# First weights split behind the first norm, longer load runs, and V's layer norm tiles in another order

## The chip, the cores and the metric

One Trainium2 chip, one of its cores. The metric is device microseconds of one execution of the program; the number given for a kernel is the median of its runs. Each core has five engines with a queue of their own: TensorE (PE, whose weight loads the profile shows apart as PEld), VectorE (DVE), ScalarE (ACT), GpSimd (POOL) and SyncE (SP, which here issues nearly all DMAs).

## What is computed

Three layers over 8 batches of 576 tokens with 512 features, all in float32:

```python
# 1. linear attention, 8 heads of 64, no softmax, then an RMS norm per head
kv  = einsum('bhsd,bhse->bhde', k, v)
out = einsum('bhsd,bhde->bhse', q, kv)
x   = out / sqrt(mean(out * out, -1) + 1e-6) * g_norm      # -> [8, 576, 512]
# 2. four experts of one causal attention head each, the best two of each token weighted
q, k, v = x @ wq[e], x @ wk[e], x @ wv[e]
a   = softmax(causal(q @ k.T / 8));  ye = a @ v @ wo[e];  x2 = sum of w[e] * ye
# 3. gated MLP with a matrix over the sequence
h   = gelu(x2 @ w_in);  u, v = h[..., :512], h[..., 512:]
v_n = (v - mean(v)) / sqrt(var(v) + 1e-6) * g_ln
out = x2 + (u * (w_sg @ v_n + b_sg)) @ w_out
```

## The kernel before

The program runs in two phases. Phase 1 does layers 1 and 2 batch by batch, phase 2 does layer 3. TensorE multiplies in fp32r, a faster format with fewer bits, so that each float32 operand that matters is split in a high part and the rest (`whi`/`wlo`, `xhi`/`xlo`), and a product is three matmuls: high by high, high by low, low by high.

The code doesn't issue instructions where it stands. A `Recorder` collects every operation, and its `plan` goes through a list schedule: it has a duration for each kind of operation (`cost`), and of the operations that are ready on an engine it takes the one with the lowest index. The index comes from `streams` and `merge`: each part of a batch (`front`, `norm`, `v`, `qk0`, `qk1`, `attn`), the split of the weights (`wld`, `wts`) and the conversions of phase 2's weights (`conv`, `conv2`) is a generator with a window, a start and an end in units of batches, in the table `OPT["w"]`. A pair in `behind` adds a dependency for the planner alone: the operation is not planned before the marked one. What comes out is one fixed order for each engine, and on the chip each engine goes through its own in that order and waits where an operand is missing. Since one helper (line 465) issues all of it, the profile is read by tiles.

The start, which is batch 0. `load` brings a pair of heads' K and V (tile `kv`, two DMAs) and Q (tile `q`), four pairs a batch; a DMA waits in SP's queue until the one eight before it has landed. `kv` multiplies K by V into `kvps`, `outT` multiplies by Q into `outps`; ACT squares that into `sq`, `stat` sums the squares over a head with a matmul into `statps`. `rstd` takes the root: ACT a logarithm and an exponential, then DVE a Newton step, in tiles `ya`, `yb`, `yc`; the result `y` is put in `rr`, whose upper 16 rows of 32 hold its high part and the lower ones the rest. `norm` spreads `rr` over the features with a matmul by zeros and ones (`bsel_sb`) into `nps`, for batch 0 twice, where the second overwrites the first; DVE multiplies it with `o`, and ACT and DVE or POOL split that into `xhi` and `xlo`. `fetch_weights` loads Q's, K's and V's weights into `wstage` in three pieces, and `split` makes `whi` and `wlo` of them. `vproj` (tile `vps`) and `qk_half` (tile `qkps`) are the projections. Batch 1's `kv` and `outT` follow.

The boundary of the phases. `Phase2.first` is merged with the end of batch 7's attention. It loads the result of phase 1 (`x`, `ends`), the two halves of `w_in` (`load_wi(1)` for V, `load_wi(0)` for U), w_sg (`weights_early`), multiplies four of V's tiles for batch 0 (`vmat`, the gelu waits) and then all U tiles of batches 0 and 1 (`upart`). A gelu is held back until the last exponential of the attention is done, since ACT needs another table for it. `rest` then makes V's gelu and layer norm, `vnorm`, of nine tiles: 0 to 3 are batch 0, 4 holds the last 64 rows of both batches, 5 to 8 are batch 1. A `vnorm` is a gelu on ACT, on DVE the statistics (tile `bs`), a subtraction (`vg`) and the rest after the split (`vn`), and on POOL the power -0.5 (`lny`). After that `spart` multiplies by w_sg, which needs tiles 0 to 4 for batch 0:

```python
for k in range(4):
    ps = self.vmat(0, k)
    (nc.vector.tensor_copy if k % 2 else nc.scalar.copy)(self.raw[:, k, :], ps)
    if k == 3:
        self.load_wi(0)
...
for k in (0, 4, 1, 5, 2, 6, 3, 7, 8):
    self.vnorm(0, k, self.raw[:, k, :] if k < 4 else self.vmat(0, k))
```

From there on phase 2 is one dense stream of matmuls to the end.

Of the kernel before, what the change touches and what calls it, by code (L numbers as in the profile page):

```python
# [27 lines left out]
F32 = mybir.dt.float32  # L28
F32R = mybir.dt.float32r
# [4 lines left out]
OP = mybir.AluOpType  # L34
# [7 lines left out]
E = 4  # L42
# [6 lines left out]
OPT = dict(ob=1, sx=0, pinq=0, dv=0, pin=1, cvb=2, xb=1, ldb=4, hp={}, n1=0, n2=0, f1=0, pa=4, sA=(), dg=0, cost=(1.01, 0.88, 1.22, 1.47, 1.28), avi=1, prb=4, ahb=4, alb=2, qkb=2, ahead=3, w={'attn': (0.177, 1.304), 'qk1': (0.038, 0.221), 'qk0': (-0.557, -0.055), 'v': (-0.518, -0.311), 'front': (-1.553, -1.219), 'norm': (-0.888, -0.788), 'conv': (-0.519, 3.66), 'conv2': (2.908, 6.876), 'wts': (-1.697, -1.585), 'u': (-0.178, 0.89), 'front_0': (-1.676, -1.565), 'v_0': (-1.282, -1.086), 'qk0_0': (-1.221, -1.003), 'qk1_0': (-0.126, -0.047), 'norm_0': (-1.418, -1.388), 'front_1': (-1.649, -1.316), 'norm_1': (-1.133, -0.89), 'v_1': (-0.728, -0.395), 'qk0_1': (-0.41, -0.088), 'wld': (-1.972, -1.907)})  # L49
# [183 lines left out]
class Recorder:  # L233
# [72 lines left out]
    def cost(self, op, outs, ins):  # L306
# [18 lines left out]
        if op.eng == "scalar":  # L325
# [148 lines left out]
class Phase1:  # L474
# [6 lines left out]
    def __init__(self, tc, late, early, ins, wts, gvd, nb):  # L481
        self.tc, self.nc, self.nb, self.gvd, self.wts = tc, tc.nc, nb, gvd, wts
        (self.qT, self.kvp, self.gn, self.wqkvg, self.woT, self.sel, self.bsel, self.mask, self.ident, self.sides) = ins
# [29 lines left out]
    def load(self, n):  # L513
# [4 lines left out]
        kv = self.ld.tile([P, 2, NQ, P], F32, name="kv", tag="kv")  # L518
        q = self.ld.tile([P, S], F32, name="q", tag="q")
        src = self.kvp[b, c]  # L520
# [3 lines left out]
        self.loads[n] = (q, kv[:, 0], kv[:, 1])  # L524
# [10 lines left out]
    def consts(self):  # L535
# [4 lines left out]
        nc.vector.memset(self.eps, 1e-6)  # L540
        self.tri = cst.tile([P, 1, E, E], F32, name="tri")
# [560 lines left out]
class Phase2:  # L1102
# [221 lines left out]
    def first(self):  # L1324
# [159 lines left out]
```

## Time and profile before

| | |
|---|---|
| Median of 3 runs | 805.79 us (805.34 to 806.64) |
| The profiled execution: its own time | 806.44 us |
| Its span, first to last instruction | 804.5 us |
| PE busy | 781.5 us, 97% of the span |
| PEld, DVE, ACT, POOL busy | 85%, 57%, 48%, 38% |
| Mean granted clock of TensorE | 0.994 |

The span is 1.94 us shorter than the execution's own time: what lies before the first and behind the last instruction. A group of instructions stands in the profile as engine, operation, output tile, input tiles, shape, how many, and busy time. In the timeline the bracket at a row's end is how long the engine stood idle before it and what ended that. Trace counts of the plain float32 matmuls (`kvps`, `outps`, `statps`, `nps`'s pairs aside) are twice the program's, as the chip does them in two passes.

### The profile page before, as it was taken

Reading aid. Unit: us, or ns where it says so; the run is one execution under the profiler, and the core shown is the slowest. Engines: PE = TensorE matmul, PEld = TensorE weight load, DVE = VectorE, ACT = ScalarE, POOL = GpSimd, SP = SyncE. Lnnn points to the kernel's source line nnn. Section 1 sums busy time; section 2 is a strip of 40 time slices with the busy share of each in tenths; the row PEclk is TensorE's granted clock in tenths of the full one; section 3 lists DMA queues with packets and bytes.
Section 4 is the critical chain, followed back from the end, with each engine's and each line's share of the span. In section 5 each row is a group of like instructions: output and inputs, shape, how many; then the busy total and the mean of one; then the engine's idle time right before and its main releaser. Section 6 shows DMA issues by size and latency. Waiting matters only on the chain.

```text
span 804.5 us, 16419 instructions
## 1 busy us (share of the span) xinstructions
PE 781.5 (97%) x5944; PEld 684.8 (85%) x5944; DVE 457.7 (57%) x1336; ACT 387.2 (48%) x1018; POOL 309.7 (38%) x419
## 2 busy tenths in 40 slices
PE   4899999999999999999998999999999999999998
PEld 3778788897998979889877898988989898989896
DVE  1767876958657577796558684443536254521230
ACT  1546675665656666676567844323423233322110
POOL 0346784747732558985113341311213121211120
PEclk9799999999999999999999999999999999999999
DMA  9989778685786788365596711203020310001002
GB/s 267 291 227 248 211 209 255 173 238 153 202 230 187 204 229 232 118 197 132 132 264 217 280 53 40 73 26 112 14 99 1 112 27 27 27 27 40 26 28 66
DMA packets 77090, 114.46 MB, mean 142 GB/s; under 512 B 13265, under 2 KB 40593, under 8 KB 77010
## 3 DMA queue, kind: packets, MB, share of 16 engines
q1 hardware_dynamic: 76866, 112.90, 48.6%
q8 instruction: 47, 0.77, 0.4%
q0 software_dynamic: 144, 0.52, 0.2%
q14 instruction: 33, 0.27, 0.1%
HBM read 58.31 MB, written 26.77 MB: 106 GB/s over the span
## 4 chain that ended last, share of the span: by engine, by line
PE 90%; DMA 3%; DVE 2%; POOL 2%; ACT 1%; SPq 1%; issue 0%; ACTq 0%; DVEq 0%; POOLq 0%
PE ps L465 44%; PE qkps L465 12%; PE vps L465 7%; PE scps L465 6%; PE tps L465 5%; PE avps L465 5%; PE outps L465 3%; PE kvps L465 2%; DMA kv<-in_kvp 2%; PE wxps L465 2%; PE nps L465 1%; PE rps L465 1%; PE statps L465 1%; SPq L465 1%; POOL xlo L465 1%; DVE vn L465 1%
## 5 line engine op out<-in xcount | busy, mean ns | idle before, releaser
L465 PE MATMUL ps<-wsh,vn 128*128 128x288 f32 x576 | 120.4, 295 | 0.7 <-ACT vn L465 0.5
L465 ACT ACTIVATE prob<-prob,small 128x128 f32<-128x128 f32 (+4 forms) x160 | 96.0, 601 | 29.7 <-DVE small L465 27.5
L465 PEld LDWEIGHTS ps<-wsh,vn 128*128 128x128 f32 x576 | 94.3, 188 | 1.9 <-ACT vn L465 0.7
L465 POOL TENSOR_TENSOR gl<-g,gh 128x512 fp32r<-128x512 f32 x32 | 41.6, 1299 | 137.7 <-ACT gh L465 94.6
L465 DVE CUSTOM_DVE_ANT_0 prob<-scps,mask_sb 128x128 f32<-128x128 f32 (+4 forms) x160 | 74.2, 469 | 18.1 <-PE scps L465 16.3
L465 POOL TENSOR_TENSOR lny<-lny,mhalf 128x1 f32<-128x1 f32 x36 | 33.8, 939 | 131.6 <-DVE lny L465 131.6
L465 PE MATMUL qkps<-xhi,whi 128*128 128x288 f32 x256 | 79.4, 310 | 0.0
L465 PE MATMUL qkps<-xlo,whi 128*128 128x288 f32 x256 | 76.4, 298 | 0.0
L465 PE MATMUL qkps<-xhi,wlo 128*128 128x288 f32 x256 | 76.4, 298 | 0.0
L465 PE MATMUL ps<-wsl,vn 128*128 128x288 f32 x256 | 75.5, 295 | 0.0
L465 PE MATMUL tps<-id_sb,prob 128*128 128x128 f32 (+2 forms) x480 | 75.3, 260 | 0.1
L465 PE MATMUL scps<-kh,qs 128*128 128x128 f32 (+2 forms) x192 | 65.0, 343 | 0.2 <-ACT aT L465 0.2
L465 PEld LDWEIGHTS tps<-id_sb,prob 128*128 128x128 f32 (+2 forms) x480 | 52.8, 137 | 10.7 <-issue 5.1
L465 PE MATMUL scps<-kl,qs 128*128 128x128 f32 (+2 forms) x192 | 59.0, 311 | 0.0
L465 DVE TENSOR_TENSOR g<-ps,u 128x288 f32<-128x288 f32 x64 | 28.9, 455 | 51.5 <-PE ps L465 50.9
L465 ACT CAST gh<-g 128x512 fp32r<-128x512 f32 x32 | 19.8, 619 | 78.5 <-DVE g L465 60.9
L465 POOL TENSOR_TENSOR xlo<-o,xhi 128x288 fp32r<-128x288 f32 x60 | 47.5, 828 | 14.0 <-ACT xhi L465 13.9
L465 PEld LDWEIGHTS qkps<-xhi,whi 128*128 128x128 f32 x256 | 48.2, 188 | 4.0 <-DVE lg L465 2.2
L465 DVE COPY aT<-tps 128x288 f32<-128x288 f32 (+5 forms) x112 | 44.0, 393 | 12.7 <-ACT aT L465 6.1
L465 PE MATMUL ps<-wo2h,gl 128*128 128x512 f32 x128 | 50.1, 391 | 0.0
L465 PE MATMUL ps<-wo2l,gh 128*128 128x512 f32 x128 | 50.0, 391 | 0.0
L465 PE MATMUL ps<-wo2h,gh 128*128 128x512 f32 x128 | 49.9, 390 | 0.0
(171 smaller groups left out, 2113.4 us busy)
## 6 DMA issues: line engine op xcount, KB each, us to landing
kv<-in_kvp SPq DMA_DIRECT2D x32, 384.0 KB, 6.6
q<-in_qT SPq DMA_DIRECT2D x32, 288.0 KB, 4.0
kh<-hiT SPq DMA_DIRECT2D x64, 144.0 KB, 2.8
kl<-loT SPq DMA_DIRECT2D x64, 144.0 KB, 3.0
out<-oev SPq DMA_DIRECT2D x32, 256.0 KB, 2.0
kv<-in_kvp SPq DMA_DIRECT2D x32, 192.0 KB, 6.7
qs<-hiT SPq DMA_DIRECT2D x32, 144.0 KB, 2.9
qs<-loT SPq DMA_DIRECT2D x32, 144.0 KB, 3.0
```

What stands on the lines that cost most here:

```text
L465: f(*[val(v) for v in op.args], **{k: val(v) for k, v in op.kw.items()})
```

## The change

The planner's table gets new windows for most parts, and its costs two corrections: an activation with a scale from a tile costs 0.1 more, and a small operation on POOL 0.9 where it was 0.55. New dependencies for the planner, `tie`: V's weights aren't split before the squares of batch 0's second half, Q's and K's not before the last multiplication of batch 0's norm. V's low parts are then all made on POOL. K and V of a pair of heads lie in DRAM so that each partition reads 3072 and 2048 bytes in a run, where it read 1536 twice and 1024 twice, and `wstage` reads one run of 4160 or 4096 where it read four of 1040 or 1024. For batch 0 `rr` holds the root's high part in all rows and a new tile `rl` its rest; the two matmuls into `nps`, of which one overwrote the other, become a sum of the two, and as `bsel_sb` counts each head twice `gh` is half of `g_sb`. `load_wi(0)` moves ahead of `weights_early`, and the order of V's tiles changes.

```diff
-OPT = dict(ob=1, sx=0, pinq=0, dv=0, pin=1, cvb=2, xb=1, ldb=4, hp={}, n1=0, n2=0, f1=0, pa=4, sA=(), dg=0, cost=(1.01, 0.88, 1.22, 1.47, 1.28), avi=1, prb=4, ahb=4, alb=2, qkb=2, ahead=3, w={'attn': (0.177, 1.304), 'qk1': (0.038, 0.221), 'qk0': (-0.557, -0.055), 'v': (-0.518, -0.311), 'front': (-1.553, -1.219), 'norm': (-0.888, -0.788), 'conv': (-0.519, 3.66), 'conv2': (2.908, 6.876), 'wts': (-1.697, -1.585), 'u': (-0.178, 0.89), 'front_0': (-1.676, -1.565), 'v_0': (-1.282, -1.086), 'qk0_0': (-1.221, -1.003), 'qk1_0': (-0.126, -0.047), 'norm_0': (-1.418, -1.388), 'front_1': (-1.649, -1.316), 'norm_1': (-1.133, -0.89), 'v_1': (-0.728, -0.395), 'qk0_1': (-0.41, -0.088), 'wld': (-1.972, -1.907)})
+OPT = dict(tie=(('sq01', 'sq01'), ('x031', 'x031')), ob=1, sx=0, pinq=0, dv=0, pin=1, cvb=2, xb=1, ldb=4, hp={}, n1=0, n2=0, f1=0, pa=4, sA=(), dg=0, cost=(1.01, 0.88, 1.22, 1.47, 1.28), avi=1, prb=4, ahb=4, alb=2, qkb=2, ahead=3, w={'attn': (0.248, 1.164), 'qk1': (0.038, 0.192), 'qk0': (-0.557, -0.049), 'v': (-0.58, -0.23), 'front': (-1.553, -1.228), 'norm': (-0.888, -0.788), 'conv': (-0.505, 3.687), 'conv2': (3.451, 7.767), 'wts': (-1.509, -1.37), 'u': (-0.178, 0.961), 'front_0': (-1.706, -1.653), 'v_0': (-1.288, -1.252), 'qk0_0': (-0.981, -0.694), 'qk1_0': (-0.126, -0.047), 'norm_0': (-1.502, -1.422), 'front_1': (-1.734, -1.311), 'norm_1': (-1.202, -0.906), 'v_1': (-0.83, -0.497), 'qk0_1': (-0.38, -0.024), 'wld': (-1.97, -1.94)})
...
-            d = (0.075 if fn == "activation" else 0.05) + 0.0009 * n
+            d = (0.075 if fn == "activation" else 0.05) + 0.0009 * n + 0.1 * isinstance(op.kw.get("scale"), Ref)
-            d = 0.7 if fn == "dma_start" else 0.12 if fn == "memset" else 0.55 if n <= 8 else (0.25 if fn in ("tensor_scalar", "scalar_tensor_tensor") else 0.1) + 0.0022 * n
+            d = 0.7 if fn == "dma_start" else 0.12 if fn == "memset" else 0.9 if n <= 8 else (0.25 if fn in ("tensor_scalar", "scalar_tensor_tensor") else 0.1) + 0.0022 * n
...
-        nc.sync.dma_start(kv[:, :, 0:3, :], src[:, 0:384].rearrange("t (p j) d -> p t (j d)", j=3))
-        nc.sync.dma_start(kv[:96, :, 3:5, :], src[:, 384:S].rearrange("t (p j) d -> p t (j d)", j=2))
+        nc.sync.dma_start(kv[:, 0 : 6 * P], self.kvp[b, c])
+        nc.sync.dma_start(kv[:96, 6 * P :], self.kve[b, c])
...
-            nc.sync.dma_start(st, self.wqkvg.rearrange("(c p) n -> p c n", p=P)[:, :, n0:n1])
+            nc.sync.dma_start(st.rearrange("p c n -> p (c n)"), self.wqkvg[:, NC * n0 : NC * n1])
...
-                self.split(st[:, c, :], self.whi[:, c, n0:n1], self.wlo[:, c, n0:n1], -0.125 if n0 == 0 else 1.0, c % 2)
+                ops = self.split(st[:, c, :], self.whi[:, c, n0:n1], self.wlo[:, c, n0:n1], -0.125 if n0 == 0 else 1.0, c % 2, n0 == 512)
+                nc.behind += zip(ops, OPT["tie"][0 if n0 == 512 else 1])
...
-            (nc.gpsimd if odd else nc.vector).tensor_tensor(l, st, h.bitcast(F32), op=OP.subtract)
+                (nc.gpsimd if odd or first else nc.vector).tensor_tensor(l, st, h.bitcast(F32), op=OP.subtract),
...
+        if st["b"] == 0:
+            nc.marks["root"] = nc.scalar.copy(self.rr, y)
+            self.rl = self.tmp.tile([P, HF], F32R, name="rl", tag="yc")
+            nc.marks["chain"] = nc.vector.tensor_tensor(self.rl, y, self.rr.bitcast(F32), op=OP.subtract)
+            return
...
-            for _ in range(1 if b else 2):
-                nc.tensor.matmul(ps, self.bsel_sb[:, c, h, :], self.rr, start=True, stop=True)
+            parts, g = ((self.rr,), self.g_sb) if b else ((self.rr, self.rl), self.gh)
+            for n, part in enumerate(parts):
+                nc.tensor.matmul(ps, self.bsel_sb[:, c, h, :], part, start=(n == 0), stop=(n == len(parts) - 1))
...
         self.load_ends(0)
         yield 0.5
+        self.load_wi(0)
         self.weights_early()
...
-            if k == 3:
-                self.load_wi(0)
...
-        for k in (0, 4, 1, 5, 2, 6, 3, 7, 8):
+        for k in (0, 1, 2, 4, 3, 5, 6, 7, 8):
```

What the planner makes of it shows in the engines' orders, at three places.

ScalarE at the start of the program (`sq` the squares, `whi` the weights' high parts, `ya` the root, `xhi` the norm's high parts). Before:

```order
L465 ACTIVATE sq<-outps 128x288 x4
L465 COPY kvs<-kvps 128x64
L465 CAST whi<-wstage 128x260 x4
L465 ACTIVATE sq<-outps 128x288 x2
L465 ACTIVATE whi<-wstage 128x256 x4
L465 ACTIVATE sq<-outps 128x288 x2
L465 CAST whi<-wstage 128x256 x4
L465 ACTIVATE ya<-statps,eps 128x288
```

and now:

```order
L465 ACTIVATE sq<-outps 128x288 x4
L465 CAST whi<-wstage 128x260 x4
L465 ACTIVATE ya<-statps,eps 128x288
L465 ACTIVATE ya<-ya 128x288
L465 CAST rr<-ya 128x288
L465 COPY kvs<-kvps 128x64
L465 CAST xhi<-o_183 128x288 x7
L465 ACTIVATE whi<-wstage 128x256 x3
```

The second four squares now stand ahead of every split, and eight of the twelve splits (Q's and K's) have moved from ahead of the root to behind the norm.

TensorE at the same place (`statps` the sums of squares, `kvps` batch 1's K by V, `nps` the spread root). Before:

```order
L465 MATMUL statps<-sq,sel_sb 32x288 x8
L465 MATMUL kvps<-kv 64x64 x20
L465 MATMUL nps<-rr,bsel_sb 128x288 x16
L465 MATMUL vps<-whi,xhi 128x260
L465 MATMUL vps<-wlo,xhi 128x260
```

and now:

```order
L465 MATMUL statps<-sq,sel_sb 32x288 x8
L465 MATMUL kvps<-kv 64x64 x10
L465 MATMUL nps<-rr,bsel_sb 128x288 x2
L465 MATMUL nps<-rl,bsel_sb 128x288 x2
L465 MATMUL nps<-rr,bsel_sb 128x288
L465 MATMUL nps<-rl,bsel_sb 128x288
```

One of batch 1's two pieces of K by V left this place for a later one, and the first matmuls of `nps` no longer need all of the root.

ScalarE at the boundary, the last head's five exponentials (`prob`), the copies of V's first tiles (`vraw`) and the change of tables. Before:

```order
L465 COPY vraw<-ps_7031 128x512
L465 COPY vraw<-ps_7056 128x512
L465 CAST wsl<-br 1x576
L465 CAST gvh<-gav 128x576
L465 ACTIVATE prob,den<-prob,small 128x128
L465 COPY aT_7101<-tps 128x3x96
L465 ACTIVATE prob,den<-prob,small 128x256
L465 CAST wsl<-br 1x576
L465 ACTIVATE prob,den<-prob,small 128x384
```

and now:

```order
L465 ACTIVATE prob,den<-prob,small 128x384
L465 COPY aT_7108<-tps 128x128
L465 ACTIVATE prob,den<-prob,small 96x480
L465 ACTIVATE prob,den<-prob,small 96x576
L465 COPY vraw<-ps_7077 128x512
L465 ACT_TABLE_LOAD
L465 ACTIVATE vg<-vraw 128x512 x2
```

The last head's exponentials now all stand ahead of the first copy of a V tile, where they stood behind two of them; the gelu `vg` follows at once.

## Rows read from the trace of the kernel before

**Rows 1.** The page, part 1: busy time, share of the span and instructions by engine.

```profile
PE 781.5 (97%) x5944; PEld 684.8 (85%) x5944; DVE 457.7 (57%) x1336; ACT 387.2 (48%) x1018; POOL 309.7 (38%) x419
```

**Rows 2.** Waits of PE, whole span: us in total, times, longest.

```profile
PE kvps L465 <- DMA kv<-in_kvp: 11.4, 5, 4.6
PE statps L465 <- ACT sq L465: 2.5, 2, 1.9
PE ps L465 <- ACT u L465: 1.4, 1, 1.4
PE ps L465 <- ACT vg L465: 1.1, 1, 1.1
PE ps L465 <- DVE u L465: 0.8, 1, 0.8
```

**Rows 3.** Timeline of DVE, 15 to 35 us: start, length, instructions, [idle before <- releaser].

```profile
18.78 0.46 DVE L465 COPY o<-outps 128x288 f32<-128x288 f32 x1 [0.79 <-PE outps L465]
...
20.57 0.72 DVE L465 TENSOR_TENSOR wlo<-wstage,whi 128x260 fp32r<-128x260 f32 x1
...
23.92 0.43 DVE L465 TENSOR_TENSOR wlo<-wstage,whi 128x256 fp32r<-128x256 f32 x1 [0.56 <-ACT whi L465]
...
26.71 0.46 DVE L465 SCALAR_TENSOR_TENSOR ya<-yb,ya 128x288 f32<-128x288 f32 x1
...
29.40 1.47 DVE L465 SCALAR_TENSOR_TENSOR o<-o,g_sb,nps 128x288 f32<-128x288 f32 x3 [0.55 <-PE nps L465]
```

**Rows 4.** Timeline of ACT, 15 to 31 us.

```profile
19.42 1.34 ACT L465 CAST whi<-wstage 128x260 fp32r<-128x260 f32 x4 [3.43 <-DMA wstage<-in_wqkvg]
20.66 0.70 ACT L465 ACTIVATE sq<-outps 128x288 f32<-128x288 f32 x2
...
22.48 0.70 ACT L465 ACTIVATE sq<-outps 128x288 f32<-128x288 f32 x2
...
24.71 0.50 ACT L465 ACTIVATE ya<-statps,eps 128x288 f32<-128x288 f32 x1
```

**Rows 5.** Timeline of PE, 16 to 34 us.

```profile
21.11 1.16 PE L465 MATMUL statps<-sq,sel_sb 128*32 128x288 f32 x12 [1.87 <-ACT sq L465]
22.93 1.47 PE L465 MATMUL statps<-sq,sel_sb 128*32 128x288 f32 x4 [0.66 <-ACT sq L465]
25.12 1.39 PE L465 MATMUL kvps<-kv 128*64 128x64 f32 x20 [0.72 <-DMA kv<-in_kvp]
27.13 1.46 PE L465 MATMUL kvps<-kv 128*64 128x64 f32 x20 [0.62 <-DMA kv<-in_kvp]
28.52 4.21 PE L465 MATMUL nps<-rr,bsel_sb 128*128 128x288 f32 x16
32.52 0.42 PE L465 MATMUL vps<-whi,xhi 128*128 128x260 f32 x1
```

**Rows 6.** Windows of 2 us: busy PE, PEld, DVE, ACT, POOL, then PEclk, DMA, GB/s.

```profile
18.00:20.00 2.00, 1.24 (x16) 0.57 (x14) 0.60 (x2) 0.58 (x2) 0.00 (x0) 1.00 1.10 351
...
24.00:26.00 2.00, 1.28 (x18) 0.92 (x18) 1.79 (x4) 1.66 (x5) 1.59 (x2) 0.50 1.10 253
...
32.00:34.00 2.00, 2.00 (x15) 2.00 (x14) 2.00 (x6) 1.43 (x4) 1.47 (x2) 0.75 1.05 322
```

**Rows 7.** The chain that ended last, 395 to 465 us: start, length, what.

```profile
417.23 5.67 PE ps L465 x24
...
429.65 0.87 ACT prob L465 x2
```

**Rows 8.** The chain that ended last, whole span.

```profile
37.38 1.44 PE vps L465 x12
...
165.63 2.33 PE kvps L465 x80
```

**Rows 9.** Groups of DVE, 430 to 470 us: count, busy us, mean ns, idle before.

```profile
L465 DVE SCALAR_TENSOR_TENSOR vg<-vg,mv,glb 128x512 f32<-128x512 f32 x9 | 6.7, 743 | 0.0
L465 DVE SCALAR_TENSOR_TENSOR vn<-vg,lny,vn 128x512 fp32r<-128x512 f32 x8 | 5.9, 744 | 3.0 <-ACT vn L465 3.0
```

More of the change, by code (lines that the diff above doesn't have):

```diff
@@ L517, in load @@
         nc = self.nc
[L518 removed]
+        kv = self.ld.tile([P, 2 * NQ * P], F32, name="kv", tag="kv")
         q = self.ld.tile([P, S], F32, name="q", tag="q")
[L520 to L522 removed]
+        nc.sync.dma_start(kv[:, 0 : 6 * P], self.kvp[b, c])
+        nc.sync.dma_start(kv[:96, 6 * P :], self.kve[b, c])
         nc.marks[f"load{n}"] = nc.sync.dma_start(q, self.qT[b, c * P : (c + 1) * P, :])
[L524 removed]
+        self.loads[n] = (q, kv)
     def small(self):
@@ L540, in consts @@
         nc.vector.memset(self.eps, 1e-6)
+        self.gh = cst.tile([P, 1], F32, name="gh")
+        nc.vector.tensor_scalar(self.gh, self.g_sb, 0.5, None, op0=OP.mult)
         self.tri = cst.tile([P, 1, E, E], F32, name="tri")
@@ L599, in kv @@
         for c in cs:
-            _, k, v = self.loads[b * NC + c]
+            kv = self.loads[b * NC + c][1]
             for j in range(NQ):
                 n = _rows(j)
-                for r in (slice(0, 64), slice(64, 128)):
-                    ops.append(nc.tensor.matmul(ps[r, c], k[:n, j, r], v[:n, j, r], start=(j == 0), stop=(j == NQ - 1)))
+                k0, v0 = (P * j, P * (j + 3)) if j < 3 else (P * (j + 3), P * (j + 5))
+                for h in (0, 64):
+                    k, v = (kv[:n, a + h : a + h + 64] for a in (k0, v0))
+                    ops.append(nc.tensor.matmul(ps[h : h + 64, c], k, v, start=(j == 0), stop=(j == NQ - 1)))
         nc.together(ops)
@@ L627, in outT @@
                 if b < 2:
[L628 removed]
+                    op = nc.scalar.activation(sqs[n][:, r], ps, AF.Square)
+                    nc.marks[f"sq{b}{p}"] = op
                     nc.vector.tensor_copy(o, ps)
@@ L1399, in fused_kernel, with record @@
         rec.trace(tc)
-def record(ctx, tc, qT, kvp, gn, wqkvg, woT, wo, w_in, g_ln, w_sg, b_sg, w_out, sel, bsel, mask, ident, sides, out):
+def record(ctx, tc, qT, kvp, kve, gn, wqkvg, woT, wo, w_in, g_ln, w_sg, b_sg, w_out, sel, bsel, mask, ident, sides, out):
     nb = qT.shape[0]
@@ L1410, in record @@
     early, late, mlp = ExitStack(), ExitStack(), ExitStack()
-    ph1 = Phase1(tc, late, early, (qT, kvp, gn, wqkvg, woT, sel, bsel, mask, ident, sides), wts, gvd, nb)
+    ph1 = Phase1(tc, late, early, (qT, kvp, kve, gn, wqkvg, woT, sel, bsel, mask, ident, sides), wts, gvd, nb)
     prep, attn = ph1.streams()
@@ L1428, in _layout @@
     pairs = lambda t: t.reshape(B, 4, 2, S, HD).transpose(0, 1, 3, 2, 4).reshape(B, 4, S, P)
+    rows = lambda t, p: t.reshape(B, 4, p, -1)
+    both = lambda a, z, p: np.concatenate([rows(pairs(t)[:, :, a:z], p) for t in (k, v)], axis=3)
+    spread = lambda w: w.reshape(NC, P, -1).transpose(1, 0, 2).reshape(P, -1)
     bits = lambda w: w.view(np.int64) if w.dtype == np.float64 else w
@@ L1444, in _layout @@
         "qT": q.transpose(0, 1, 3, 2).reshape(B, D, S),
-        "kvp": np.stack([pairs(k), pairs(v)], axis=2),
+        "kvp": both(0, 384, P),
+        "kve": both(384, S, 96),
         "gn": np.tile(inputs["g_norm"], 2).reshape(P, 1),
         "wqkvg": np.concatenate(
-            [heads(inputs["moe_wq"]), heads(inputs["moe_wk"]), heads(inputs["moe_wv"]), inputs["moe_w_gate"]], axis=1
-        )[order],
-        "woT": inputs["moe_wo"].reshape(E * HD, D).T,
+            [
+                spread(w[order])
+                for w in (
+                    heads(inputs["moe_wq"]),
+                    heads(inputs["moe_wk"]),
+                    np.concatenate([heads(inputs["moe_wv"]), inputs["moe_w_gate"]], axis=1),
+                )
+            ],
+            axis=1,
+        ),
+        "woT": spread(inputs["moe_wo"].reshape(E * HD, D).T),
         "wo": inputs["moe_wo"].reshape(E * HD, D),
```

20 lines of the change are left out of this document (11 added, 9 removed).

## The prediction

> **What bounds the kernel now.** I read the page first. TensorE is busy 781.5 us of the span of 804.5 [rows 1], so whatever this change does to the other engines can pay only where TensorE stands still: at most 23.0 us, and no edit takes a matmul away. The waits of TensorE, read next, say where that is: 11.4 us on the first loads of K and V, 2.5 us in the sum of squares, which waits for ACT, and 1.4, 1.1 and 0.8 us on three evacuations of V's and U's tiles at the boundary of the phases [rows 2]. Together that is 17.2 us; most of the other 5.8 lies before the first matmul and behind the last. So I read two stretches closely, the first 34 us and 395 to 465 us, and leave the rest as it is.
>
> In the first stretch the reader should follow one result from engine to engine. Batch 0's last products were there at 18.78, when DVE began to copy them [rows 3]. ACT squares the same products, but in its order V's weights come first: it waited 3.43 us for them, cast four pieces from 19.42, squared two halves at 20.66, cast Q's weights, and squared the last two from 22.48 [rows 4]. The sum of squares on TensorE stood 1.87 us and then 0.66 us for that and ended at 24.40 (22.93 + 1.47) [rows 5]; the root began at 24.71 [rows 4], its last Newton step ended at 27.17 [rows 3]. TensorE meanwhile multiplied two pieces of batch 1's K by V, each behind a wait for its load, and began to spread the root at 28.52 [rows 5]. DVE multiplied the first piece at 29.40 [rows 3], and the first projection began at 32.52 [rows 5]. The granted clock was half, 1.2 GHz, in 24 to 26 us and back at 2.4 GHz inside 32 to 34 us [rows 6].
>
> In the second stretch the chain of waits leaves TensorE at 429.65, with the last exponential [rows 7]. Before that, 24 matmuls of V's first tiles took 5.67 us from 417.23 on [rows 7], ahead of the last head's scores: they put off the end of the exponentials, and so the table change and every gelu.
>
> **Part 1, the splits behind the norm.** Q's and K's eight casts on ACT and their subtractions leave the path to the root. Four squares in a row take 1.4 us (two take 0.70 [rows 4]); from 18.8 that is about 20.3 with the wait for the second half's products. From the start of the last pair of squares to the end of the sums it took 1.92 us (22.48 to 24.40) [rows 4, 5]. The last pair now starts at about 19.6, so the sums end at 21.5, which is 2.9 us sooner. V's four casts (1.34 us [rows 4]) still stand between squares and root on ACT; they end near 21.7 if the weights land as now, so the root starts at 21.8, as 0.31 us behind the sums was the case before. From there to the first multiplied piece it took 4.69 us (24.71 to 29.40) [rows 3, 4], which gives 26.5. The cast and one subtraction in place of cast, scaling and sum may save 0.4 more; I leave it out.
>
> This part has a price. V's low parts now all go to POOL, at the time at which DVE does the Newton step. A DVE subtraction beside POOL took 0.72 us, one alone 0.43 [rows 3]. Four DVE operations with two inputs stand in the root's chain now, so it costs between 0 and 4 x 0.29 = 1.2 us. I take 0.4: POOL's work begins when the first cast is done and should be mostly over by the last two steps. First multiplied piece by this chain: 26.9.
>
> Q's and K's splits cost nothing where they are now, as their first reader stands behind all five of V's tiles: 5 x 1.44 = 7.2 us [rows 8] cover eight casts at 1.34 us for four [rows 4]. If they were late, the first Q projection would be, by what is missing.
>
> **Part 2, the loads.** The spread of the root still stands behind one piece of batch 1's K by V on TensorE. With the loads as they are that piece ends at 26.51 (25.12 + 1.39) [rows 5], and the first multiplied piece follows the spread's start by 0.88 us (28.52 to 29.40) [rows 3, 5]: 27.4. So the loads would bind, not the root, unless the longer runs help. Does the trace price a run's length? In all windows of this stretch the DMA engines are fully busy; where mostly weights moved, in runs of 1 KB, it was 351 GB/s, and with K and V in runs of 1.5 and 1 KB 253 [rows 6]. The shorter runs weren't slower. The bounds are 0 and, if the 7.8 us up to 25.12 went at 351 in place of 253 GB/s, 2.2 us. I take 0.5, close to the lower end, because the rows show no gain from length.
> The Trainium skill, DMA: Bandwidth & Descriptors, Specifications, has it that a transfer needs 512 bytes at least for the line rate. The runs of K, V and the weights have 1024 bytes or more on both sides of the change; by that rule the longer ones bring nothing, and the sum below would be 0.5 us less of a gain. The row above agrees more than not, which is why the rule is a rival of its own below.
>
> Both ways meet at 26.9, so the norm starts 2.5 us sooner than at 29.40. What left this place returns: one piece of K by V, at the full clock 2.33 / 4 = 0.6 us [rows 8]. The spread itself is paced by DVE, so half the clock costs nothing there. For the projections I assume that the clock comes back as long after the spread's start as it did: then nothing is lost. Start: 2.5 - 0.6 = **1.9 us** gained, with ends of 0 and 4.
>
> **Part 3, V's tiles and w_in.** The 5.67 us of V's matmuls now stand behind the last head's scores instead of ahead of them, so the gelus can start up to that much sooner, while TensorE still has V's and U's matmuls to do. Each tile costs DVE a subtraction of 0.743 and a rest of 0.744 us besides the statistics [rows 9], and batch 0 now needs the first five in the list where the old list put its last at the seventh place. U's half of w_in is issued ahead of w_sg, so U's matmuls don't wait for it; w_sg is four DMAs later and has until the first product with it, behind all of U's. Of the 3.3 us of evacuation waits [rows 2], I take back 2.6. What stays: in DVE's new order three of those operations stand in a row, 2.2 us, ahead of a copy that frees a bank, and TensorE has about two tiles in the meantime. Bounds: the whole 3.3 gained, or 1 lost, if the last head's steps, which lost their cover, make TensorE wait for the exponentials.
>
> **Part 4, the table.** The new windows move conversions to later batches and narrow the attention. The waits of rows 2 lie at the start and the boundary, none in the 300 us between, so there is less than 1 us to win there; to lose, a wait of the size of the smallest (0.8) once or twice. I take 0.
>
> **The sum**, against the profiled execution's own time of 806.44 us (its span and 1.94 us around it): 806.44 - 1.9 - 2.6 = 801.9. That execution lies 0.65 us over the median of the runs, 805.79, so for the median 801.3 us.
>
> **The rivals.**
> Better than that: POOL is out of DVE's way and K and V land 2 us sooner, so the norm starts near 25.4, and all three evacuation waits go. Then 805.79 - (4.0 - 0.6) - 3.3 = 799.1. For it speaks that nothing else in rows 3 to 5 stands in the path; against it that the loads bind as soon as the root doesn't.
>
> The loads stay as they are, by the rule cited, and the slow clock stays to the same moment. The norm then starts at 27.4, 2.0 us sooner, the first projection at 30.5, and up to 33.0 it runs at half speed and loses 1.25 us. The start is worth 2.0 - 0.6 - 1.25 = 0.15 us, and with 2.6 at the boundary the time is 803.0. For it: rows 6.
>
> The change doesn't do at the boundary what the new list is for: the same evacuations wait behind other DVE and POOL work. Then only the start's 1.9 us come: 803.9.
>
> Slower: the last head. V's 24 matmuls were cover for it, and the loads of x and of V's half of w_in are issued only after the last Q and K projection. If TensorE gets through the last head's scores before these have landed, or waits at each step for DVE and ACT, it loses up to what it did there before, 5.67 us [rows 7], and the gelus come no sooner: 805.79 - 1.9 + 5.67 = 809.6. It decides the sign once it costs more than the 1.9 us of the start. Against it: in rows 2 no wait of TensorE for those loads shows, and the exponentials do move ahead.
>
> **How the numbers follow.** A measurement of this kernel tells about 0.2%, 1.6 us, from no change: faster is below 804.2, slower above 807.4. Forecast 0.52, better 0.16, loads and clock 0.14, boundary as before 0.10, slower 0.08. The three faster cases and most of the two weak ones (0.14 + 0.10, which lie 1.2 and 0.3 us inside the line, so a part of them counts as no change) give 0.78 faster, 0.14 the same, 0.08 slower. The predicted time is the forecast's, 801.3. The range reaches from 798.4, where the upper ends of parts 1 to 3 lie (805.79 - 4.0 - 3.3 = 798.5), over both weak cases to 804.6.
>
> **What would show it.** Right: no ACT cast of Q's or K's weights ahead of the logarithm; the sums of squares end near 21.5, the first multiplied piece near 26.9 and the first projection near 30; TensorE's waits for evacuations below 1 us in all; the first gelu several us nearer to the last V product of the attention. Wrong, if TensorE's wait for K and V stays at 11 us with the spread at 26.5 or later, if the granted clock is still half at 32 us, or if a wait for `xh`, `wih` or `prob` turns up at the boundary.

## The result, and the profile after

The changed kernel took 795.9 us (median of 4 runs, 794.06 to 797.83) beside 805.71 before: a ratio of 0.9877, 95% interval 0.985 to 0.9903. That is faster by 9.8 us where 4.5 were forecast, and outside the range (798.4 to 804.6). In a later comparison the same kernel had 794.28 beside 805.42 (0.9857, 0.9842 to 0.9872), so the two figures set how finely other versions can be told from it: about 1.6 us. The profiled execution took 795.16 us, its span is 793.4.

The page, part 1, and the waits of PE of the changed kernel (us in total, times, longest):

```profile
PE 773.6 (98%) x5944; PEld 682.7 (86%) x5944; DVE 459.0 (58%) x1334; ACT 385.2 (49%) x1018; POOL 309.0 (39%) x421
```

```profile
PE kvps L465 <- DMA kv<-in_kvp: 12.4, 4, 5.0
PE scps L465 <- DVE gav L465: 0.6, 1, 0.6
PE outps L465 <- DVE o L465: 0.5, 1, 0.5
PE statps L465 <- DVE o L465: 0.5, 1, 0.5
PE nps L465 <- ACT rr L465: 0.4, 1, 0.4
```

The three waits for u and vg [rows 2] are gone, and so is the one for the squares; the wait for K and V has even grown from 11.4 to 12.4. But idle time fell by 3.2 us only (23.0 to 19.8), and busy time by 7.9, for the same matmuls: much of what was won had been counted as busy. So I made a second account. For each matmul I took the time to the start of the next one on TensorE; the median of a shape behind 36 us, over both kernels, is its undisturbed price. What a stretch takes beyond the sum of these prices is its lost time. Where the matmuls of a shape run in groups side by side, the median leaves out the one long step of each group, so the figures contain regular work as well, and only differences between versions count:

| Stretch, us | before | changed | won |
|---|---|---|---|
| to 36: start, batch 0 | 26.8 | 23.1 | 3.7 |
| 36 to 100: batch 1 | 11.9 | 9.8 | 2.1 |
| 100 to 400 | 24.5 | 25.0 | -0.5 |
| 400 to 480: boundary | 9.2 | 3.3 | 5.9 |
| 480 to the end | 0.9 | 1.0 | -0.1 |

The sum, 11.1 us, is the difference of the two spans. The start, in the timelines of PE, ACT and DVE of the changed kernel, 18 to 29 us:

```profile
19.34 1.18 PE L465 MATMUL statps<-sq,sel_sb 128*32 128x288 f32 x16 [0.49 <-DVE o L465]
22.99 1.09 PE L465 MATMUL kvps<-kv 128*64 128x64 f32 x20 [2.47 <-DMA kv<-in_kvp]
24.48 0.85 PE L465 MATMUL nps<-rr,bsel_sb 128*128 128x288 f32 x2 [0.40 <-ACT rr L465]
...
28.35 0.36 PE L465 MATMUL vps<-whi,xhi 128*128 128x260 f32 x1
```

```profile
18.38 1.32 ACT L465 ACTIVATE sq<-outps 128x288 f32<-128x288 f32 x4 [2.58 <-PE outps L465]
19.56 1.36 ACT L465 CAST whi<-wstage 128x260 fp32r<-128x260 f32 x4
20.79 0.53 ACT L465 ACTIVATE ya<-statps,eps 128x288 f32<-128x288 f32 x1
...
24.00 0.43 ACT L465 CAST rr<-ya 128x288 fp32r<-128x288 f32 x1 [2.21 <-DVE ya L465]
```

```profile
21.83 0.74 DVE L465 TENSOR_TENSOR yc<-ya 128x288 f32<-128x288 f32 x1
22.61 0.87 DVE L465 SCALAR_TENSOR_TENSOR yb<-yc,yb 128x288 f32<-128x288 f32 x1
23.51 0.46 DVE L465 SCALAR_TENSOR_TENSOR ya<-yb,ya 128x288 f32<-128x288 f32 x1
...
25.62 1.36 DVE L465 SCALAR_TENSOR_TENSOR o<-o,gh,nps 128x288 f32<-128x288 f32 x3 [0.70 <-PE nps L465]
```

Each piece answers to one in rows 3 to 5: the sums end at 20.52 where they ended at 24.40, the root begins at 20.79 instead of 24.71, one piece of K by V stands ahead of the spread where there were two, and the spread begins at 24.48 instead of 28.52. The first projection starts at 28.35 instead of 32.52. The granted clock is back sooner too, in windows of 2 us of the changed kernel (columns as in rows 6):

```profile
24.00:26.00 2.00, 1.60 (x10) 1.52 (x7) 0.83 (x2) 0.54 (x2) 0.00 (x0) 0.61 1.04 314
26.00:28.00 2.00, 2.00 (x11) 2.00 (x10) 2.00 (x6) 1.47 (x4) 0.89 (x1) 0.53 1.05 301
28.00:30.00 2.00, 2.00 (x17) 1.83 (x17) 2.00 (x6) 1.64 (x5) 1.39 (x3) 1.00 1.06 256
```

It was half (1.2 GHz) from 24.5 to 27.9, where it had been half from 22.8 to 33.0; in both, TensorE had stood in waits before it fell. But this moves from one execution to the next: in the profile of the later comparison it was half from 22.1 to 28.9, and that execution took 795.05 us beside 795.16.

At the boundary, ACT's timeline of the changed kernel: the last exponential, the table change and the first gelus.

```profile
417.27 0.78 ACT L465 ACTIVATE prob<-prob,small 96x576 f32<-96x576 f32 x1 [0.26 <-DVE small L465]
...
418.63 1.28 ACT L465 ACT_TABLE_LOAD   x1
419.92 1.15 ACT L465 ACTIVATE vg<-vraw 128x512 f32<-128x512 f32 x2
```

The exponential that came at 429.65 [rows 7] now comes at 417.27, some 5 us of which are the program's head start by then. Windows of 20 us there, of the kernel before and then of the changed one: TensorE's busy time goes from 18.94 and 17.70 to 19.69 and 20.00.

```profile
420.00:440.00 20.00, 18.94 (x126) 15.31 (x124) 14.88 (x42) 13.32 (x29) 4.40 (x5) 1.00 0.71 239
440.00:460.00 20.00, 17.70 (x125) 16.95 (x125) 13.40 (x30) 16.14 (x32) 7.47 (x9) 1.00 0.66 233
```

```profile
420.00:440.00 20.00, 19.69 (x149) 17.50 (x148) 16.44 (x39) 14.91 (x31) 4.09 (x6) 1.00 0.57 181
440.00:460.00 20.00, 20.00 (x136) 19.00 (x135) 13.74 (x32) 12.77 (x26) 9.02 (x9) 1.00 0.90 318
```

### The profile page after: what moved, and what is told of

Same layout as the page of the kernel before. It is cut to its first block, busy times and chain, and to the rows that moved or that the text cites. A ratio compares the mean times of both kernels' runs of the same rounds, so it can differ in the third digit from the quotient of the medians.

```text
span 793.4 us, 16453 instructions
## 1 busy us (share of the span) xinstructions
PE 773.6 (98%) x5944; PEld 682.7 (86%) x5944; DVE 459.0 (58%) x1334; ACT 385.2 (49%) x1018; POOL 309.0 (39%) x421
## 4 chain that ended last, share of the span: by engine, by line
PE 88%; DMA 4%; DVE 3%; POOL 2%; ACT 1%; SPq 1%; issue 0%; POOLq 0%; ACTq 0%
PE ps L465 46%; PE qkps L465 12%; PE vps L465 7%; PE scps L465 6%; PE tps L465 5%; PE avps L465 5%; PE kvps L465 2%; PE outps L465 2%; PE wxps L465 2%; PE nps L465 1%; DMA q<-in_qT 1%; PE rps L465 1%; DMA xh<-gvh 1%; SPq L465 1%; DMA kv<-in_kve 1%; PE statps L465 1%
## 5 line engine op out<-in xcount | busy, mean ns | idle before, releaser
L465 ACT ACTIVATE prob<-prob,small 96x576 f32<-96x576 f32 (+4 forms) x160 | 95.7, 599 | 11.4 <-DVE small L465 10.7
L465 POOL TENSOR_TENSOR lny<-lny,mhalf 128x1 f32<-128x1 f32 x36 | 32.0, 892 | 135.2 <-DVE lny L465 135.2
L465 PE MATMUL tps<-id_sb,prob 128*128 128x128 f32 (+2 forms) x480 | 72.2, 260 | 0.2 <-DVE small L465 0.2
L465 PEld LDWEIGHTS tps<-id_sb,prob 128*128 128x128 f32 (+2 forms) x480 | 51.1, 137 | 11.9 <-issue 6.3
L465 ACT CAST gh<-g 128x512 fp32r<-128x512 f32 x32 | 19.8, 618 | 80.5 <-DVE g L465 62.8
L465 DVE COPY oev<-ps 128x512 f32<-128x512 f32 (+1 forms) x20 | 12.8, 638 | 73.1 <-PE ps L465 57.3
L465 POOL TENSOR_TENSOR xlo<-o,xhi 128x288 fp32r<-128x288 f32 x60 | 46.9, 819 | 10.2 <-ACT xhi L465 7.4
L465 DVE COPY aT<-tps 128x288 f32<-128x288 f32 (+5 forms) x112 | 43.9, 393 | 11.8 <-PE tps L465 5.8
```

The lines of the kernel that those rows point to most:

```text
L465: f(*[val(v) for v in op.args], **{k: val(v) for k, v in op.kw.items()})
```

## Experiments

All were measured beside the kernel before; its median was 805.35 to 805.61 throughout. "Lost" is the account above. The theory at the outset: each of the three stretches wins by itself, the start through the sooner root and the longer runs.

**The two halves.** One run keeps the start's parts of the change alone, the other the rest. The planner's windows were divided accordingly.

> The kernel before with the start's parts of the change alone: the layout of the loads, the ties, the two products of the root, V's low parts on GpSimd, the start's windows (batch 0 and 1 and the weights); the other windows, costs, V's order and w_in's place as before. Theory: the start is worth 4.7 us up to 36 us and some 1.5 us more in batch 1's norm and mode changes up to 100 us: 799.5 to 801.5 us. Rival: the start is worth what I forecast, 1.9 us, and the rest belongs to the boundary and the middle: 803.5 to 804.5 us.

> The kernel before with the other half: the later batches' and phase 2's windows, the costs, V's order and w_in's place; loads, root, ties and the start's windows as before. Theory: the boundary is worth about 5 us: 800 to 801.5 us, and with the start alone the two gains add up to the whole 9.8 us. Rival: it is worth my 2.6 us: 803 us, and the two together leave some 3 us that come only with both.

Measured: 803.63 us (ratio 0.9968, 0.9957 to 0.9979) for the start and 799.87 (0.9925, 0.9912 to 0.9938) for the rest. By the total the start is worth 2.0, as my rival had it, but the account says otherwise: it won 5.3 us up to 36 and 1.5 up to 100, and lost 2.5 between 100 and 400, where the old windows follow the new start (27.0 lost against 24.5). The account flatters it: the profiled execution, 802.03 us, is one of two fast ones out of six, 1.6 us under the median. The largest single wait there, TensorE's for VectorE's copy of aT at 317 us, is only 1.0. By the medians the two halves add up to 7.7 us, where the whole won 9.8 or 11.1; by the spans of the profiles to 9.8 of 11.1. What is missing may be the new middle windows, which keep what the start wins: the whole lost no more between 100 and 400 than the kernel before, but no run changed them alone. The rest won 4.7 of its 5.7 at the boundary (lost 4.5 against 9.2), as the theory had it.

**What the start hangs on.** Three versions of the changed kernel: without the ties, with the old root, and with the old order of one pair of pieces.

```diff
-                nc.behind += zip(ops, OPT["tie"][0 if n0 == 512 else 1])
```

> The changed kernel without the ties: the planner puts the weights' splits ahead of and between the squares and the root again (seven of the eight casts of Q's and K's weights ahead of the logarithm), two products of the root, loads and windows kept. Theory: the ties carry the start: the root starts some 2.5 us later than at 20.79, the norm's first piece is near 28 us, 798 to 799.5 us. Rival: the norm is bound by batch 1's K and V (TensorE waited 2.47 us for them up to 22.99), so at most 0.5 us comes back: 796 to 796.8 us.

```diff
-        if st["b"] == 0:
-            nc.marks["root"] = nc.scalar.copy(self.rr, y)
...
-            parts, g = ((self.rr,), self.g_sb) if b else ((self.rr, self.rl), self.gh)
...
+            for _ in range(1 if b else 2):
+                nc.tensor.matmul(ps, self.bsel_sb[:, c, h, :], self.rr, start=True, stop=True)
```

> The changed kernel with batch 0's root in one tile again: cast, scaling and sum ahead of the first matmul of the spread, the same matmul issued twice; ties, loads and windows kept. Theory: one more VectorE operation (0.46 us) and the wait for all of the root put the norm's first piece 0.7 to 1 us later: 796.5 to 797.2 us. Rival: the third piece of K by V ends at 24.08 and covers it: within 0.4 us of the changed kernel's 795.9.

```diff
...
+                if b == 0:
+                    nc.behind.append((op, "kvm11"))
```

> The changed kernel with one dependency more for the planner: batch 0's spread of the root isn't planned before the second piece of batch 1's K by V, as it stood before the change. Ties, two products, loads and windows kept. Theory: what the ties and the two products are worth comes by way of this: with either undone the planner put both pieces ahead of the spread, each behind its load (24.1 and 25.4 where the second began), and 2.4 to 2.9 us came back; so 797.8 to 799 us with all else in place. Rival: what they are worth is the shorter root itself, and a second piece in TensorE's waiting time costs nothing: 796 to 796.8 us.

Measured: 798.78 (0.9919, 0.9906 to 0.9931), 798.30 (0.9908, 0.9895 to 0.9921) and 798.88 us (0.9921, 0.9906 to 0.9936): 2.4 to 4.6 us slower than the changed kernel's two medians. The old root was expected at 796.5 to 797.2; it costs as much as the others. What the three have in common is the order on TensorE. PE's timeline with the old root:

```profile
19.20 1.18 PE L465 MATMUL statps<-sq,sel_sb 128*32 128x288 f32 x16 [0.49 <-DVE o L465]
23.61 1.34 PE L465 MATMUL kvps<-kv 128*64 128x64 f32 x20 [3.24 <-DMA kv<-in_kvp]
25.41 1.33 PE L465 MATMUL kvps<-kv 128*64 128x64 f32 x20 [0.45 <-DMA kv<-in_kvp]
26.67 3.75 PE L465 MATMUL nps<-rr,bsel_sb 128*128 128x288 f32 x16
30.40 0.36 PE L465 MATMUL vps<-whi,xhi 128*128 128x260 f32 x1
```

Both pieces of K by V stand ahead of the spread again, each behind its load. In the third run a dependency of the spread on the second piece's last matmul ("kvm11") forces that order, with everything else of the change in place, and by the medians the price is the same. So the sooner root pays by letting the plan put the spread ahead of the second piece. Up to 36 us that is the smaller part: there the three lost 0.7, 1.4 and 2.9 us more than the changed kernel, and the 2.9 are from the slowest of six executions (801.83). All three also lost about 12.2 us between 36 and 100, as the kernel before did (11.9), where the versions with one piece lost 9.8 to 10.4: with it batch 1's norm comes at another place, and the plain float32 matmuls of that stretch (K by V, by Q, the sums) lie in 7 or 8 runs between other work instead of 10 (11 before). The number of these runs goes with the loss more closely than the piece does: the last version below has one piece ahead of the spread and 10 runs, and lost 12.0. That they are the cause isn't shown.

**The length of the runs.** The old layout of K, V and the weights, once in the changed kernel and once with V's list put back (below); no engine's order moves.

```diff
-        nc.sync.dma_start(kv[:, 0 : 6 * P], self.kvp[b, c])
...
+        nc.sync.dma_start(
+            kv[:, 0 : 6 * P].rearrange("p (t m) -> p t m", t=2), src[:, 0:384].rearrange("t (p j) d -> p t (j d)", j=3)
+        )
...
-            nc.sync.dma_start(st.rearrange("p c n -> p (c n)"), self.wqkvg[:, NC * n0 : NC * n1])
+            nc.sync.dma_start(st, self.wqkvg.rearrange("(c p) n -> p c n", p=P)[:, :, n0:n1])
```

> The changed kernel with the old layout of K, V and the Q, K, V weights in DRAM (runs of 1024 to 1536 bytes), every engine's order as in the changed kernel. Theory: the long runs themselves are worth about 2 us, since in the profile of the changed kernel batch 1's first K and V landed at 22.85 where they landed at 24.98 before, and the wait of the third piece of K by V for them is the last wait ahead of the norm: 797 to 799 us, the norm's first piece near 27 us instead of 25.62. Rival, by the Trainium skill's rule that I cited (DMA: Bandwidth & Descriptors): 1024 bytes are as good as 3072, the loads come sooner only because the queue is issued sooner, and the time stays within 0.8 us of the changed kernel's.

> The changed kernel with the list of V's tiles put back (the best so far, 794.25) and the old layout of the loads with it. Theory: batch 1's first K and V land 1.8 us later with the short runs (24.3 in both profiles of kernels with short runs and windows of after or before, 21.7 to 23.6 with the long ones), and TensorE waits for them in this order: 795.5 to 796.5 us. Rival: the time doesn't show it, as it didn't in the changed kernel (796.1 to 795.9): within 0.6 us of 794.25.

Measured: 796.10 us (0.9882, 0.9869 to 0.9895) beside the changed kernel's 795.9 and 794.28, and 796.31 (0.9882, 0.9868 to 0.9897) beside 794.25. The first came as its rival had it, the second as its theory had it. The windows from 14 to 20 us, of the changed kernel and of the one with short runs, where mostly the weights move:

```profile
14.00:20.00 6.00, 4.55 (x75) 2.70 (x72) 3.00 (x9) 3.04 (x11) 0.00 (x0) 1.00 1.03 374
```

```profile
14.00:20.00 6.00, 4.42 (x70) 2.60 (x66) 2.60 (x7) 2.76 (x10) 0.51 (x1) 1.00 1.09 327
```

The eight profiles with short runs have 318 to 327 GB/s there, the nine with long runs and the old place of `bsel_sb` (three versions below move it) 353 to 393; the second pair has 319 and 385. So the rate is some 15% higher, with the DMA engines just as full. The start shows it too: with the short runs the first piece of K by V ended at 25.88 instead of 24.08, and the norm's first piece came at 26.93 and 27.34, where the five profiles with long runs and the same start have 24.66 to 26.26. In the whole time it is 0.2 to 2.1 us, hardly more than these runs can tell.

**The boundary.** First the list and w_in's place in the changed kernel, together and apart.

```diff
-        for k in (0, 1, 2, 4, 3, 5, 6, 7, 8):
+        for k in (0, 4, 1, 5, 2, 6, 3, 7, 8):
...
-        self.load_wi(0)
         self.weights_early()
...
+            if k == 3:
+                self.load_wi(0)
```

> The changed kernel with V's tiles in the old order (0, 4, 1, 5, 2, 6, 3, 7, 8) and U's half of w_in loaded behind V's fourth tile, windows kept. The last head's exponentials then still stand ahead of all but one of V's copies on ScalarE. Theory: at the boundary the gain (the loss of TensorE between 420 and 480 us fell from 6.4 to 1.0 us) comes from the new windows, which let the exponentials and with them the gelus go first; then this kernel loses at most 1.5 us: 796 to 797.5 us. Rival, as my prediction had it: the list of V's tiles and the earlier w_in carry it, and 2.6 us or more come back: 798.5 us or more, with TensorE waits for vg, u or vn of over 2 us in the profile.

> The changed kernel with only the list of V's tiles put back (0, 4, 1, 5, 2, 6, 3, 7, 8); TensorE's order is that of the changed kernel, only the tables of ScalarE and VectorE at the boundary move. Theory: of the 4.5 us that the list and w_in's place carry together, the list has little, because the waits that came back (3.2 us for vg) stood where U's matmuls had no w_in to start with: 796 to 797 us. Rival: the list carries it, since batch 0's last tile stands at the seventh place again: 798.5 us or more, with TensorE waits for vn or vg of over 2 us.

> The changed kernel with only U's half of w_in put back behind V's fourth tile and w_sg. Theory: this carries the boundary: w_in landed at 420.5 in the changed kernel's profile and at 432.9 with the late place, so that U's matmuls can't lie between V's and TensorE waits for the gelus instead: 799.5 to 801 us. Rival: w_in's place is worth under 1 us: 796 to 797 us.

> The changed kernel itself, beside the others of this call. Theory: 795 to 797 us, so that the old list of V's tiles (794.25) is better by 1 to 2 us; rival: the two are one and the same within 0.6 us, 794 to 794.9 us.

Measured: both back, 800.44 us (0.9934, 0.992 to 0.9947); the list alone, 794.25 (0.9861, 0.9846 to 0.9876); w_in alone, 800.88 (0.9942, 0.9927 to 0.9957); nothing, 794.28. So my theory of the windows fell at once (796 to 797.5 expected with both back), and the list counts for nothing here. With w_in late, 9.0 us are lost at the boundary as before, although the table change stays at 418.6. PE's timeline with w_in late:

```profile
437.25 0.40 PE L465 MATMUL ps<-xh,wih 128*128 128x288 f32 x1 [4.10 <-ACT vg L465]
```

Its issues of U's half of w_in, and below them those of the changed kernel (timeline of SP's queue): 6 us apart, with w_sg between.

```profile
419.75 1.06 SPq L465 DMA_DIRECT2D wih<-wd0h  x2
420.85 1.66 SPq L465 DMA_DIRECT2D wil<-wd0l  x2
```

```profile
413.49 2.31 SPq L465 DMA_DIRECT2D wih<-wd0h  x2
416.37 1.18 SPq L465 DMA_DIRECT2D wil<-wd0l  x2
```

All of V's matmuls then run in one block, until V's tiles fill the banks (the buffers that matmuls write) and TensorE waits for their gelus. Behind this wait the granted clock was half from 438.1 to 441.5 us, while it was full at the boundary of the kernel before and of the changed one; the matmuls in that stretch took 1.7 us more than their price. So w_in's place seemed to carry the boundary. Four runs then added it to the kernel before: alone, with the attention's window, with the list, and with both. (They keep the changed kernel's longer runs for wo's weights, one load issued at 34 us, as the two halves above do.)

> The kernel before with one edit alone: U's half of w_in is loaded ahead of w_sg and not behind V's fourth tile (everything else as before, the planner's table too). Theory: this one edit carries the boundary, 4 to 5 us: 800.5 to 802 us, with under 1 us of TensorE waits for vg, u and vn left. Rival: without the new windows the exponentials stay behind V's tiles and the gelus late, so the earlier w_in finds no use: 804.5 us or more.

> The kernel before with two edits: U's half of w_in early, and of the planner's windows the attention's alone as in the change (0.248 to 1.164 in place of 0.177 to 1.304). ScalarE's order then has all but the last exponential ahead of the first copy of a V tile. Theory: the early w_in pays only where U's matmuls don't go ahead of the last head's scores (alone they did, the table change came at 441.1 in place of 430.7 and TensorE stood 5.6 us for vn); with the attention ending first it is worth the boundary's 5 us: 800 to 801.5 us. Rival: the other windows (conversions, U's) are needed too: 803.5 us or more.

> The kernel before with U's half of w_in early and the new list of V's tiles; the planner's table as before. Theory: the list takes away the wait for the norm of batch 0's last tile (5.6 us for vn where w_in alone was moved), though the change of tables stays late (441): 804 to 806.5 us. Rival: as the gelus start 10 us later than before, the list can't help: 808.5 us or more.

> The kernel before with U's half of w_in early, the new list of V's tiles and the attention's window; all other windows and the costs as before. Theory: the three together carry the boundary, as in the run of the boundary's half alone (799.9): no wait for vn over 1 us and 420 to 480 us lose under 2 us against TensorE's rate; the middle lost 4 us more with this window alone (100 to 400 us), so 802.5 to 804.5 us in all. Rival: the other windows decide there too, the wait for vn stays at 4 us: 808 us or more.

Measured: 810.71 us (1.0061, 1.0049 to 1.0073), 810.73 (1.0065, 1.0052 to 1.0079), 808.29 (1.004, 1.0026 to 1.0055) and 805.42 (0.9996, 0.9987 to 1.0004). The theory fell in the first two: the edit that is worth 5 us in the changed kernel costs 5 in the kernel before. ACT's timeline and PE's waits with w_in alone:

```profile
441.13 1.28 ACT L465 ACT_TABLE_LOAD   x1
442.43 0.64 ACT L465 ACTIVATE vg<-vraw 128x512 f32<-128x512 f32 x1
```

```profile
PE ps L465 <- ACT vn L465: 5.6, 2, 3.6
```

and its windows of 10 us behind that:

```profile
450.00:460.00 10.00, 5.92 (x24) 5.19 (x25) 6.15 (x13) 6.72 (x13) 4.22 (x5) 0.73 0.66 230
460.00:470.00 10.00, 8.01 (x44) 7.78 (x44) 9.80 (x25) 6.51 (x12) 3.55 (x4) 0.76 1.05 387
```

U's matmuls, whose operands are there early, are planned ahead of the last head's scores; the table change comes at 441.1, the layer norm late, and TensorE stands before w_sg. The waits are only a part of the price: TensorE stood 6.3 us at the boundary instead of 4.1, but with the waits the clock fell to half, for 10.2 us in all (454.5 to 461.3 and 464.8 to 468.2), and the matmuls there took 4.4 us more than their price. So most of the 5 us is the clock's. The attention's window alone brings the table change back to 433.3 but loses 4 us between 100 and 400, and batch 0's last tile is still late:

```profile
PE ps L465 <- ACT vn L465: 4.0, 1, 4.0
```

Here the list helps. With it that wait is gone, and the boundary loses 6.6 us instead of 10.7, 1.5 of it still at half the clock. The middle still loses 4. Both runs with the list missed what I had expected (804 to 806.5 and 802.5 to 804.5): with the list and the old window the table change stays at 440.9, a wait of 5.0 us for vn is left, and the boundary loses 11.8. So the boundary's 5.9 us belong to no single edit. The windows alone (w_in late) win nothing there, w_in alone loses 5; together they win it, without the list as well (794.25). Where the gelus come later the list takes back a part: 4 us with the table change at 432 to 433, 2.5 with it at 441. Which of the other windows, or the two corrected costs, makes the difference between 805.4 (both, and the list) and the 799.9 of the second half isn't shown.

**The bytes ahead of batch 1.** Three tries at a faster version: `bsel_sb`, 0.5 MB, issued at the very start and read by the spread, is loaded later. In the first GpSimd issues it behind two of V's low parts, in the others behind a multiplication of a column `x` of batch 0's third K, which waits for that load. The last also loads Q's and K's weights behind batch 1's first pairs.

```diff
-        nc.gpsimd.dma_start(self.bsel_sb, self.bsel)
+        nc.marks["late"] = nc.gpsimd.tensor_tensor(t, x, x, op=OP.mult)
+        nc.behind.append((nc.gpsimd.dma_start(self.bsel_sb, self.bsel), "late"))
```

> The changed kernel with the list of V's tiles put back, and the zeros and ones of the spread (bsel_sb, 0.5 MB) no longer loaded at the program's start but issued by GpSimd behind the first two low parts of V's weights. Theory: the DMA engines are full up to 24 us and these 0.5 MB lie ahead of K, V and the weights, so that all of these land some 1.5 us sooner (0.5 MB at the 350 GB/s of those windows): the squares end near 18.2, the norm's first piece near 24.3, 793 us or less. Rival: the late 0.5 MB share the engines with batch 1's loads and land behind 25, and the spread waits for them: 795 us or more.

> The changed kernel with the old list of V's tiles, and bsel_sb's 0.5 MB issued by GpSimd when the third K and V of batch 0 have landed (a multiplication of one column of them stands ahead of the issue); order of the other engines as in the changed kernel's start. Theory: they land some 8 us behind an issue near 11.5, at 20, ahead of the spread; batch 0's K and V land 1.5 us sooner and the root with them, while batch 1's first K and V land as now (22.9): the norm's first piece 0 to 0.7 us sooner, 793.5 to 794.5 us. Rival: nothing is won since batch 1's K and V bind: 794.5 us or more.

> As bsel_mid, and Q's and K's weights (1 MB, first read by splits near 30 us) are loaded behind batch 1's first pairs. Theory: batch 1's first K and V then land near 20 in place of 22.9, TensorE no longer waits for them (2.5 us) and the norm is bound by the root alone: the norm's first piece near 24.3, 792 to 793.5 us. Rival: Q's and K's weights land too late for their splits and the first Q projection waits: 795 us or more.

Measured: 807.78 us (1.0029, 1.0019 to 1.004), 794.82 (0.9863, 0.9849 to 0.9876) and 803.25 (0.9971, 0.9962 to 0.9981). None came as its theory had it. The first fails by its own load, which landed 8.4 us after its issue (27.8 us lost up to 36), PE's timeline:

```profile
28.86 0.58 PE L467 MATMUL nps<-rr,bsel_sb 128*128 128x288 f32 x1 [3.80 <-DMA bsel_sb<-in_bsel]
```

The second is no better than the changed kernel. The third is as good up to 36 us (23.0 lost) and loses 2 us in batch 1 and 6 at the boundary, where nothing had been touched. PE's waits of the third:

```profile
PE ps L465 <- ACT vn L465: 4.0, 1, 4.0
PE nps L465 <- ACT rr L465: 1.6, 1, 1.6
```

The first has the same 4.0 us for vn, and in both the clock fell to half at the end of that wait, for 3.4 us; that is some 1.5 us of the loss. Both have V's old list, and the plan of the boundary had come out otherwise: the table change is at 430.2 and 423.6 us, where the changed kernel has it at 418.6. No version beat the changed kernel by more than the runs can tell.

## Why the prediction was wrong, point by point

The sign and the places were right: the squares ahead of the splits, the spread behind one piece, the gelus earlier. The first step failed: "whatever this change does to the other engines can pay only where TensorE stands still". Of the 11.1 us by which the profiled span fell, idle time was 3.2 and busy time 7.9, since waits delay more than they show, the clock counts as busy, and matmuls paced by another engine count as busy too. So the terms were too small, 1.9 for the start where 3.7 came and 2.6 for the boundary where 5.9 came, and batch 1's 2.1 us stood in the sum as 0.

- **Part 1, the root.** The sums ended at 20.52, not 21.5. The squares began at 18.38, not 18.8, so that the last pair came at 19.0, not 19.6; and from there to the end of the sums it took 1.5 us, not 1.92, a figure from a stretch at half the clock: four sums took 1.47 us there [rows 5, 6], sixteen at the full clock 1.18. The root began at 20.79, not 21.8. The price of POOL beside DVE was 0.7 us (0.74 and 0.87 where 0.46 is usual), not 0.4, inside its bounds. The norm's first piece came at 25.62, 3.8 us sooner than before, where I had 2.5.
- **Part 2, the loads.** I took 0.5 us of a range up to 2.2; the piece of K by V ended at 24.08, 2.4 us sooner than 26.51, and 1.8 us sooner than with the short runs. "The rows show no gain from length" compared stretches with different transfers; with the order held still, the rate was 374 and 327 GB/s. The Trainium skill's rule, DMA: Bandwidth & Descriptors, Specifications, which sees the line rate from 512 bytes on, does not agree with this row. The rival with the loads as they were, 803.0 us, did not come.
- **The clock.** That it "comes back as long after the spread's start as it did" was too cautious for this profile: the windows above put it back 3.4 us behind the start (half up to 27.9), not 4.5. That was partly luck: in the profile of the later comparison it is 3.9 us behind a spread that began at 25.00. Together the start won 3.7 us to 36, where I had 1.9 and an upper end of 4.0.
- **Part 3, the boundary.** "Bounds: the whole 3.3 gained" was no upper end. Rows 2 left out two waits of PE for vn, 0.5 and 0.2 us, and each wait delays the next matmul by some 0.16 us more than its idle time: that of 1.42 us put off the next by 1.59. The five waits' delay was 4.8 us; 5.9 were won in all, and where the other 1.1 come from stays open. The reason I gave, the list and w_in, was half right: w_in needs the windows (810.7 without), the list isn't needed (794.25).
- **Part 4, the table.** "Less than 1 us to win" between the ends fell on batch 1, 36 to 100 us, where 2.1 were won without a wait in the list: four matmuls of its norm were paced by VectorE in the kernel before (0.37 to 0.51 us from one to the next, where 0.13 is usual: some 1.2 us), and the small-tiled matmuls lay in more runs. No run took these two apart.
- **The rivals.** The better one, 799.1, was the nearest. The slower one, the last head without cover, didn't come; the runs with w_in alone show that a late last head does cost 5 us here, most of it by the clock that fell with the waits.

## What to carry to other kernels

Where a planner writes the order, an edit's worth is that of the new order, not of the edit: look for the one or two instructions that changed places on the bound engine, and force just these. Test each part both ways, taken from the new kernel and added to the old one; here the same line was worth +5 and -5 us. And bound a gain by the engine's time against its own undisturbed rate, not by its idle time; a duration from a stretch at half the clock is not one for the full clock, and a wait has to be priced with the granted clock that follows it.

## What was not expected of the hardware

With the DMA engines full in both cases, the load rate rose from 318 to 327 GB/s with runs of 1 to 1.5 KB to 353 to 393 with runs of 2 to 4 KB (14 to 20 us). And a DMA from GpSimd's queue, issued at 20.3 us, landed 8.4 us later, much as those of SP's queue did (medians of 6.8 to 8.6 us in the changed kernel between 10 and 30 us): here a second queue brought it no sooner. Last, the clock at the boundary: in the profiles of eight versions, in which TensorE's longest wait there was 1.5 to 5.0 us, it fell to half at about the end of a wait, for 3.4 to 10.2 us in all, and the matmuls in these stretches took 1.5 to 4.4 us more than their price. In the kernel before and the changed one it stayed full.
